# A gated MLP in sums and differences: raw groups and their sums in one tile, signs moved, and some loads placed elsewhere

## The chip, the cores and the metric

The kernel runs on one core of a Trainium2 chip. The time is the device time of one execution in microseconds. A core has five engines that run side by side and wait for each other by semaphores: TensorE (PE, matmuls, with its weight loads PEld), VectorE (DVE), ScalarE (ACT), GpSimd (POOL) and SyncE (SP). SP, ACT and POOL start DMA transfers. Each engine works through its instructions in a fixed order; an instruction that waits holds up all that stand behind it on its engine.

## The reference

```python
x = A_u                                               # 2048 tokens x 576
sa, ca, ga, sb, cb, gb = silu(c) @ w_mod              # six rows of 576
h = layernorm(x) * (1 + ca) + sa
x = x + ga * ssm(h)                                   # long convolution over the tokens
h = layernorm(x) * (1 + cb) + sb
z = gelu(h @ w_in)                                    # 576 -> 4608
z1, z2 = z[:, :2304], layernorm(z[:, 2304:])
g = w_sp @ z2 + b_sp[:, None]                         # 2048 x 2048, over the tokens
x = x + gb * ((z1 * g) @ w_out)                       # 2304 -> 576
```

The convolution and the layer norms stand as in the reference. The change is in the second half, from `z` on.

## The kernel before, in words

**Stages.** The first 440 us compute the convolution; its result is x1, kept in device memory as `x1_d`, 16 blocks of 128 rows. Phase A (`phase_a`, about 440 to 694 us) makes z2 for all 2048 tokens, normalises it and stores it as `z2_d`; it also splits `w_in` into float16 parts (`win_d`) and prepares seven of the eight blocks of `w_sp` for the first quarter. Phase B (`phase_b`, to the end) goes through four quarters q of 512 tokens. A quarter has nine steps f. Each makes z1 for 256 of the 2304 columns (`z1_unit` in quarter 0; `z1_pair` in quarters 1 to 3) and then `g = w_sp @ z2` for the same columns (`g_products`), whose result `g_unit` multiplies by z1. After the ninth step `out_block` multiplies by `w_out` in eight halves (four blocks of rows, two halves of columns), adds x1 and stores the rows.

**Seven products in place of eight.** A matrix product is cut into 2 x 2 parts and done as seven products of sums and differences of the parts. So each operand needs seven pieces: four raw groups or three of them, and sums. Each piece is split into two float16 numbers, a high part and a remainder, and three products of these are added: 21 matmuls for a pair of operand tiles. `z2_build` makes a set of z2 (`zset`), `wsp_build` a block of `w_sp` (`wsp`), `n2_build` the rows of the layer norm (`n2o`), and `wa_unit` a set of `w_in` (`zset` again, quarter 1; quarters 2 and 3 load what quarter 1 stored in `wa_d`). Each of them loads four groups of 256 columns into a tile `raw` (four buffers of 4 KB a partition), makes three or four sums on DVE into a tile `sum` (two buffers), and splits raw groups and sums apart: ACT scales to the high part, DVE subtracts it for the remainder. `w_sums` and `z_sums` are the sums. Sets of z2 that a later quarter needs are stored in `set_d` by ACT and loaded by POOL.

**w_in's last rows.** 512 of the 576 rows go through the seven products; the last 64 take six plain matmuls with a tile `wr`. In quarter 0 `z1_unit` scales them from its tile `wf` (three buffers) into a tile `ot` with an ACT copy (L1468), stores them in `wr_d` by ACT (L1470), and `wa_unit` loads them in the later quarters.

**Order.** In phase B the order of the instructions on PE and SP is that of the program. On DVE and ACT it is chosen when the kernel is built, except in the handover after each quarter's ninth step (`self.nc = self.last`), where the builds for the next quarter (`n2_build`, `wsp_build`, and `g_unit` of step 8) keep program order on DVE and ACT too. `ahead` is called at each new set: it builds two sets further on, with raw loads three ahead, and in quarter 0 loads and splits a piece of `w_out`. A load into a buffer waits on SP until the last user of that buffer is done, and SP's later loads wait behind it. In the handover SP's order is: rows for `n2_build`, blocks of `w_sp` as raw buffers come free, the bias row, the first sets of the next quarter, and last the rows of x1 (L1582 on), which take raw buffers too.

Line 129 is that of a helper which records all instructions that keep program order, so the trace tells these apart by their tiles. A program's tile `z1` is called `z` in the trace, `z2_d` is `z_d`, `x1_d` is `x_d`.

Of the kernel before, what the change touches and what calls it, by code (L numbers as in the profile page):

```python
# [765 lines left out]
class Mlp:  # L766
    def __init__(self, tc, ctx, I, x1_d, dram, mod_d, acc, out):
# [7 lines left out]
        self.wr_d = dram.tile([9, 128, 2, 2, 128], F16, name="wr_d")  # L775
# [67 lines left out]
    def start(self):  # L843
# [9 lines left out]
        self.sc = mc.tile([128, 96], F32, name="sc")  # L853
# [83 lines left out]
    def scales_sp(self, q, ps=None):  # L937
# [5 lines left out]
        V.tensor_scalar(qcol(q, INV_SP), qcol(q, I_S), 1.0 / 256, None, op0=ALU.mult)  # L943

# [66 lines left out]
    def wsp_load(self, q, i, pool):  # L1011

        t = self.wss[i] = self.bp.tile([128, 4, 256], F32, name="raw", bufs=4) if pool is None else self.norm_tile(pool).rearrange("p (k n) -> p k n", k=4)
        self.wsp_read(t, q, i)
# [11 lines left out]
    def w_sums(self, r, z):  # L1026
        V = self.nc.vector
        V.tensor_tensor(z[:, 0], r[:, 0], r[:, 1], op=ALU.subtract)
        V.tensor_tensor(z[:, 2], r[:, 2], r[:, 0], op=ALU.subtract)
        V.tensor_tensor(z[:, 1], r[:, 2], z[:, 0], op=ALU.subtract)  # L1030
        V.tensor_tensor(z[:, 3], r[:, 3], z[:, 1], op=ALU.subtract)

    def z_sums(self, r, z):
        V = self.nc.vector
        V.tensor_tensor(z[:, 1], r[:, 2], r[:, 0], op=ALU.subtract)
        V.tensor_tensor(z[:, 0], r[:, 1], z[:, 1], op=ALU.add)
        V.tensor_tensor(z[:, 2], r[:, 3], z[:, 1], op=ALU.subtract)

    def raw(self, key):
        t = self.wss[key] = self.bp.tile([128, 4, 256], F32, name="raw", bufs=4)  # L1040
        return t

# [9 lines left out]
    def wsp_sums(self, i):  # L1052
        t = self.wss["b", i]
        self.w_sums(t[:, :4], t[:, 4:])

    def wsp_hi(self, q, i):
        self.hi(self.wsp_tile(q, i)[:, :, 0], self.wss["b", i][:, 1:], self.qcol(q, S_S), act=True)

    def wsp_lo(self, q, i):
        o = self.wsp[q, i]  # L1060
        self.lo(o[:, :, 1], self.wss.pop(("b", i))[:, 1:], self.qcol(q, S_S), o[:, :, 0])


    def wsp_build(self, q, i):
        r = self.wss.pop(("b", i))
        o = self.wsp_tile(q, i)
        z = self.bp.tile([128, 4, 256], F32, name="sum", bufs=2)
        self.w_sums(r, z)
        for t, k in ((r[:, 1:], slice(0, 3)), (z, slice(3, 7))):
            self.split(o[:, k, 0], o[:, k, 1], t, self.qcol(q, S_S), act=True)  # L1070

    def z2_load(self, n):
        self.nc.sync.dma_start(self.raw(("a", n)), self.z2_d[n // 4, n % 4].rearrange("p s g c -> p s (g c)"))

    def z2_build(self, n):
# [4 lines left out]
        z = self.bp.tile([128, 4, 256], F32, name="sum", bufs=2)  # L1080
        self.z_sums(r, z)
        for t, k in ((r, slice(0, 4)), (z[:, :3], slice(4, 7))):
            nc.scalar.activation(o[:, k, 0], t, AF.Copy)  # L1083
            nc.vector.tensor_tensor(o[:, k, 1], t, o[:, k, 0], op=ALU.subtract)  # L1084
# [20 lines left out]
    def roots(self, z=None, x=None):  # L1105
# [10 lines left out]
        if z is not None:  # L1116
            r2 = ap.tile([128, 1], F32, name="r2")
            nm = ap.tile([128, 1], F32, name="nm2")
            V.tensor_scalar(r2, r[:, 1:2], 256.0, None, op0=ALU.mult)
# [250 lines left out]
    def n2_load(self, q, j):  # L1370
# [4 lines left out]
        t = self.n2t[j] = self.raw(("n", j)).rearrange("p k n -> p (k n)").bitcast(F16).rearrange("p (t m c) -> p t m c", t=4, m=4)  # L1375
        self.nc.sync.dma_start(t, self.n2_d[q][:, :, j:8:2])

    def n2_build(self, q, j):

        V, t, o = self.nc.vector, self.n2t.pop(j), self.n2o[q][j]  # L1380
        r = self.bp.tile([128, 4, 256], F32, name="sum", bufs=2)
        for h in range(2):
            V.tensor_tensor(r[:, 2 * h:2 * h + 2].rearrange("p k (t c) -> p (k t) c", c=128), t[:, :, h], t[:, :, 2 + h], op=ALU.add)
        z = self.bp.tile([128, 4, 256], F32, name="sum", bufs=2)
        self.w_sums(r, z)
        for u, k in ((r[:, 1:], slice(0, 3)), (z, slice(3, 7))):
            self.split(o[:, k, 0], o[:, k, 1], u, 0.25, act=True)

    def wa_raw(self, f):
        t = self.raw(("w", f)).rearrange("p (s h) (j c) -> p s h j c", h=2, j=2)  # L1390
# [5 lines left out]
    def wa_unit(self, q, f):  # L1396

        nc, V = self.nc, self.nc.vector
        wr = self.wrs[f] = self.fp.tile([128, 2, 2, 128], F16, name="wr", bufs=2)
# [392 lines left out]
```

## Time and profile before

| What | us |
|---|---|
| three runs | 1803.0, 1799.34, 1793.21 |
| their median | 1799.34 |
| the profiled execution | 1795.97 |
| its span, first to last instruction | 1794.2 |

Busy time of the engines in five stretches of the profiled execution, in us:

| Stretch | length | PE | DVE | ACT | granted clock |
|---|---|---|---|---|---|
| convolution, 0 to 440 | 440.0 | 356.6 | 360.4 | 323.5 | 0.94 |
| phase A, to 693.8 | 253.8 | 241.6 | 231.0 | 165.8 | 0.96 |
| quarter 0, to 925.6 | 231.8 | 223.2 | 192.9 | 122.4 | 0.99 |
| its output and the handover, to 987.6 | 62.0 | 55.5 | 51.2 | 22.8 | 0.94 |
| quarters 1 to 3, to the end | 806.6 | 801.9 | 442.2 | 207.8 | 1.00 |

The granted clock is TensorE's, as a share of full speed. A row of the timeline has the start in us, the length, the engine (a `q` behind it: its queue, where it starts a DMA), the line, the operation, the tile written and the tiles read, the shape, and how many equal ones were merged; in brackets how long the engine stood idle before it and what ended that. A row of the groups has the count, the busy time, the mean in ns, and the idle time before.

### The profile page before, as it was taken

To read this page: it belongs to the slowest core of one execution; us is meant where nothing else is said; L and a number is where in the kernel's file an instruction comes from. 1 tells how busy PE (TensorE), PEld (TensorE's weight loads), DVE (VectorE), ACT (ScalarE), POOL (GpSimd) and SP (SyncE) were. 2 spreads that over 40 slices of the span, in tenths; PEclk is the share of its full clock that TensorE was granted. 3 is DMA by queue.
4 is the path that set the end of the run, shared out by engine and by line. 5 is a ranking of instruction groups with operands and counts; after the bars stand their busy time and mean duration, and the time that the engine had idled before them with its cause. 6 is when DMAs were issued, how large, how long until landed. Compare 5 with 4: busy or idle time off the path is not lost.

```text
span 1794.2 us, 35815 instructions
## 1 busy us (share of the span) xinstructions
PE 1678.7 (94%) x14766; PEld 1251.7 (70%) x14766; DVE 1277.5 (71%) x2522; ACT 842.3 (47%) x1130; POOL 237.5 (13%) x376
## 2 busy tenths in 40 slices
PE   2588999998899998999998999999999999999998
PEld 1244555565455544877786888888888888888887
DVE  8876999966999996989798576778344468344432
ACT  2668999954577665555443343334122123111110
POOL 3311222333122211000000000000111100111100
PEclk9789999998999999999999999999999999999999
DMA  9465746679689888877664787874666573556630
GB/s 250 122 215 183 193 120 172 179 206 305 205 263 280 240 233 241 294 270 256 234 196 155 236 279 269 289 258 129 218 229 211 199 247 106 197 194 209 222 104 27
DMA packets 184757, 378.22 MB, mean 211 GB/s; under 512 B 37681, under 2 KB 105265, under 8 KB 183825
## 3 DMA queue, kind: packets, MB, share of 16 engines
q1 hardware_dynamic: 138384, 157.31, 30.3%
q0 software_dynamic: 36128, 171.57, 29.0%
q10 hardware_dynamic: 10080, 47.04, 6.6%
q8 instruction: 116, 1.90, 0.5%
q14 instruction: 49, 0.39, 0.1%
HBM read 263.94 MB, written 102.49 MB: 204 GB/s over the span
## 4 chain that ended last, share of the span: by engine, by line
PE 55%; DVE 14%; DMA 6%; issue 4%; ACT 3%; POOL 0%; SPq 0%; ACTq 0%; DVEq 0%; POOLq 0%
PE ps L129 49%; PE pz L129 2%; DVE zset L1084 2%; DVE bsz L129 1%; DMA wf<-win_d 1%; DVE n L129 1%; DVE wso L129 1%; DVE wsp L129 1%; DVE rq L129 1%; DVE sum L129 1%; ACT zset L1083 1%; PE pk L487 1%; DMA wst<-in_w_in 1%; DMA wsst<-in_w_out 1%; DVE gt L1517 1%
## 5 line engine op out<-in xcount | busy, mean ns | idle before, releaser
L129 PEld LDWEIGHTS <-zset 128*128 128x128 f16 x7182 | 703.3, 98 | 88.5 <-DVE zset L1084 2.4
L129 PE MATMUL ps<-wsp,zset 128*128 128x256 f16 x6048 | 667.8, 273 | 4.0 <-DVE zset L1084 2.1
L129 PE MATMUL pz<-wz,nt 128*128 128x512 f16 (+1 forms) x1120 | 224.6, 361 | 9.3 <-DVE nt L129 5.0
L129 PEld LDWEIGHTS <-nt 128*128 128x128 f16 x1120 | 109.9, 99 | 117.9 <-issue 7.0
L1517 DVE SCALAR_TENSOR_TENSOR gt<-ps,sc,bsp 128x512 f32<-128x512 f32 x32 | 24.0, 749 | 231.1 <-PE ps L129 231.1
L129 PE MATMUL ps<-wout,z 128*128 128x288 f16 x1344 | 172.3, 288 | 6.5 <-ACT ot L1566 5.7
L1479 POOL DMA_DIRECT2D zset<-set_d x96 | 51.1, 532 | 882.1 <-PE ps L129 594.6
L129 PEld LDWEIGHTS <-z 128*128 128x128 f16 x1344 | 132.5, 99 | 41.1 <-issue 7.0
L1444 ACT ACTIVATE z<-ps 128x256 f32<-128x256 f32 x42 | 13.9, 382 | 245.4 <-PE ps L129 245.4
L129 PE MATMUL ps<-n2o,zset 128*128 128x256 f16 x1134 | 128.2, 273 | 0.0
L1517 DVE SCALAR_TENSOR_TENSOR gt<-ps,sc,gt 128x512 f32<-128x512 f32 (+1 forms) x160 | 108.4, 695 | 4.6 <-DVE gt L1517 0.5
L1084 DVE TENSOR_TENSOR zset<-raw,zset 128x1024 f16<-128x1024 f32 x48 | 58.6, 1221 | 40.0 <-ACT zset L1083 40.0
L1441 DVE TENSOR_TENSOR z<-ps,z 128x512 f32<-128x512 f32 (+1 forms) x126 | 71.9, 597 | 12.5 <-PE ps L129 9.9
L1083 ACT ACTIVATE zset<-raw 128x1024 f16<-128x1024 f32 x48 | 50.2, 1049 | 58.5 <-PE ps L129 26.3
L129 PE MATMUL ps<-n2q,wf 128*128 128x512 f16 x252 | 57.1, 386 | 4.7 <-DMA wf<-win_d 4.7
L395 DVE SCALAR_TENSOR_TENSOR ft<-ft,ps 128x1024 f32<-128x1024 f32 x36 | 43.8, 1218 | 20.8 <-ACT ft L394 20.8
L129 ACT ACTIVATE z<-pz,sc 128x512 f32<-128x512 f32 (+1 forms) x96 | 52.1, 583 | 11.6 <-PE pz L129 6.1
L1567 DVE TENSOR_TENSOR ot<-ot,ps 128x288 f32<-128x288 f32 x32 | 14.3, 451 | 55.0 <-ACT ot L1566 55.0
L129 ACT ACTIVATE z<-z,nm,r 128x1152 f32<-128x1152 f32 x24 | 31.5, 1342 | 44.4 <-DVE nm L129 27.9
L129 PE MATMUL ps<-wout,z1b 128*128 128x288 f16 x384 | 52.3, 286 | 0.0
L1566 ACT ACTIVATE ot<-ps 128x288 f32<-128x288 f32 x32 | 12.7, 405 | 84.1 <-PE ps L129 67.9
L445 PEld LDWEIGHTS pk<-small,kab 128*64 128x64 f32 x576 | 32.6, 139 | 26.7 <-issue 16.6
(359 smaller groups left out, 2772.5 us busy)
## 6 DMA issues: line engine op xcount, KB each, us to landing
zset<-set_d POOLq DMA_DIRECT2D x96, 896.0 KB, 5.0
set_d<-zset ACTq DMA_DIRECT2D x36, 896.0 KB, 6.4
raw<-z_d SPq DMA_DIRECT2D x48, 512.0 KB, 4.3
raw<-in_w_spT SPq DMA_DIRECT2D x43, 512.0 KB, 5.3
z_d<-z POOLq DMA_DIRECT2D x32, 576.0 KB, 9.5
zset<-wa_d POOLq DMA_DIRECT2D x18, 896.0 KB, 4.9
u_d<-st1o POOLq DMA_DIRECT2D x16, 576.0 KB, 4.7
u<-u_d SPq DMA_DIRECT2D x36, 256.0 KB, 4.7
```

The source lines that it names most:

```text
L129: return self.tc.keep_in_program_order(f(*a, **k))
L395: V.scalar_tensor_tensor(f, f, MAGIC, pa, op0=ALU.subtract, op1=ALU.subtract)
L445: T.matmul(pm[64 * ri:64 * ri + 64, 128 * i:128 * i + 128], kk[:, i], r1[ri], start=True, stop=True, skip_group_check=True)
L487: T.matmul(pm, fwd, u1, start=True, stop=True)
L1083: nc.scalar.activation(o[:, k, 0], t, AF.Copy)
L1084: nc.vector.tensor_tensor(o[:, k, 1], t, o[:, k, 0], op=ALU.subtract)
L1441: V.tensor_tensor(dst, pm, to, op=ALU.add)
L1444: A.activation(g1[:, k], p17[:, 0], AF.Copy)
L1479: self.nc.gpsimd.dma_start(o, self.set_d[n // 4, n % 4])
L1517: V.scalar_tensor_tensor(dst, pm, inv, to, op0=ALU.mult, op1=ALU.add)
L1566: A.activation(ot, pl, AF.Copy, scale=1.0 / 2048)
L1567: V.tensor_tensor(ot, ot, pa, op=ALU.add)
```

## The change

- `raw` holds seven groups (three buffers of 7 KB); the sums are made in the same tile, behind or among the raw groups, and the tile `sum` is gone. The high part and the remainder of all seven are made by one ACT and one DVE instruction each, not two.
- The sums are cut to two or three instructions, one of them 512 wide. For this some pieces have the opposite sign: the norm of even blocks of z2 multiplies by -256 instead of 256, and `g_unit` uses a negative scale (`NEG_SP`) in two of its additions. The list of products is one for all (`PRODUCTS`), with the same number of matmuls.
- w_in's last rows: `z1_unit` no longer scales and stores them, `wr_d` is gone. `wr_load` reads them from `win_d` one step ahead, and `wr_scale` scales them in place on ACT (two copies a step) in quarters 1 to 3.
- Rows of x1 go into a tile of their own, `xo`, and into the buffer of `gt`, in turn. In quarters 0 to 2 the first three blocks of rows are loaded from the handover on, ahead of the next quarter's first sets on SP; `w_out`'s even pieces go through `xo` as well.
- Order: at the start of phase B the eighth block of `w_sp` is loaded and built first. In the handover the first n2 load and the first block come one set later and only one block, not three, is loaded then; `n2_build` of the second half comes after block 0, not after block 2.

```diff
+    def w_sums(self, r):
         V = self.nc.vector
+        V.tensor_tensor(r[:, 4:6], r[:, 1:3], r[:, 0:1].to_broadcast([128, 2, 256]), op=ALU.subtract)
+        V.tensor_tensor(r[:, 0], r[:, 2], r[:, 4], op=ALU.add)
+        V.tensor_tensor(r[:, 6], r[:, 3], r[:, 0], op=ALU.subtract)
+    def z_sums(self, r):
         V = self.nc.vector
+        V.tensor_tensor(r[:, 4], r[:, 2], r[:, 0], op=ALU.add)
+        V.tensor_tensor(r[:, 5:7], r[:, 1:4:2], r[:, 4:5].to_broadcast([128, 2, 256]), op=ALU.subtract)
     def raw(self, key):
-        t = self.wss[key] = self.bp.tile([128, 4, 256], F32, name="raw", bufs=4)
+        t = self.wss[key] = self.bp.tile([128, 7, 256], F32, name="raw", bufs=3)
         return t
+    def half(self, key, k):
+        b = self.bp
+        t = self.wss[key] = (b.tile([128, 2, 512], F32, name="gt", bufs=1).rearrange("p h n -> p (h n)") if k else b.tile([128, D], F32, name="xo"))[:, :D]
+        return t
...
     def wsp_build(self, q, i):
         r = self.wss.pop(("b", i))
         o = self.wsp_tile(q, i)
-        z = self.bp.tile([128, 4, 256], F32, name="sum", bufs=2)
-        self.w_sums(r, z)
-        for t, k in ((r[:, 1:], slice(0, 3)), (z, slice(3, 7))):
-            self.split(o[:, k, 0], o[:, k, 1], t, self.qcol(q, S_S), act=True)
+        self.w_sums(r)
+        self.split(o[:, :, 0], o[:, :, 1], r, self.qcol(q, S_S), act=True)
...
     def z2_build(self, n):
...
-        z = self.bp.tile([128, 4, 256], F32, name="sum", bufs=2)
-        self.z_sums(r, z)
-        for t, k in ((r, slice(0, 4)), (z[:, :3], slice(4, 7))):
-            nc.scalar.activation(o[:, k, 0], t, AF.Copy)
-            nc.vector.tensor_tensor(o[:, k, 1], t, o[:, k, 0], op=ALU.subtract)
+        self.z_sums(r)
+        nc.scalar.activation(o[:, :, 0], r, AF.Copy)
+        nc.vector.tensor_tensor(o[:, :, 1], r, o[:, :, 0], op=ALU.subtract)
...
     def n2_build(self, q, j):
...
-        r = self.bp.tile([128, 4, 256], F32, name="sum", bufs=2)
+        r = self.raw(("m", j))
...
+    def wr_load(self, f):
+        wr = self.wrs[f] = self.fp.tile([128, 2, 2, 128], F16, name="wr", bufs=2)
+        self.nc.sync.dma_start(wr.rearrange("p h k c -> p h (k c)"), self.win_d[f:f + 10:9, :, 8:10].rearrange("h p k c -> p h (k c)"))
+    def wr_scale(self, f):
+        for h in range(2):
+            w, b = self.wrs[f][:, h], R_C + (f + 9 * h) // 4
+            self.nc.scalar.activation(w, w, AF.Copy, scale=self.col(b))
...
     def z1_unit(self, q, f):
...
-        nc.scalar.activation(self.wr0[:, h], w[:, 8:], AF.Copy, scale=self.sc[:, R_C + b:R_C + b + 1])
-        if h == 1:
-            nc.scalar.dma_start(self.wr_d[f % 9], self.wr0)
...
     def g_unit(self, q, f, pg, parts=1):
...
-        add(g1, both(p17[:, 0]), self.bsp[q])
+        add(g1, both(p17[:, 0]), self.bsp[q], neg)
...
-        add(g2, both(p17[:, 1]), g2)
+        add(g2, both(p17[:, 1]), g2, neg)
...
     def wout_load(self, f):
-        t = self.bp.tile([128, D], F32, name="gbs") if f % 2 else self.raw(("out", f)).rearrange("p k n -> p (k n)")[:, :D]
+        t = self.half(("out", f), 0) if f % 2 == 0 else self.bp.tile([128, D], F32, name="gbs")
...
+    def rows_load(self, q, tt):
+        self.nc.sync.dma_start(self.half(("x", tt), tt % 2), self.x1_d[4 * q + tt])
     def out_block(self, q):
...
             if h == 0:
-                xts[tt] = self.raw(("x", tt)).rearrange("p k n -> p (k n)")[:, :D]
-                S.dma_start(xts[tt], self.x1_d[4 * q + tt])
+                if tt > 2 or q == 3:
+                    self.rows_load(q, tt)
...
-            if f == 8 and q < 3 and i == 0:
-                block(q + 1, 3)
+            if f == 8 and q < 3 and i == 1:
+                self.n2_load(q + 1, 0)
+                block(q + 1, 1)
+                self.rows_load(q, 0)
...
-        more(0, AHEAD)
-        self.wsp_read(self.raw(("b", 7)), 0, 7)
-        ready(0, 1)
+        self.wsp_read(self.raw(("b", 7))[:, :4], 0, 7)
+        more(0, 2)
+        self.wsp_build(0, 7)
         for i in range(3, 6):
             self.z1_load(0, order[i])
         ready(0, 2)
-        self.wsp_build(0, 7)
...
                 pg = self.g_products(q, f)
+                if q and f < 8:
+                    self.wr_scale(f + 1)
...
                 if q < 3:
-                    if i == 3:
+                    if i == 1:
                         self.n2_build(q + 1, 1)
                     self.wsp_build(q + 1, i)
-                    block(q + 1, i + 4)
+                    block(q + 1, i + 3 if i > 1 else i + 2)
+                    if i == 1:
+                        self.rows_load(q, 1)
+                        block(q + 1, 4)
             self.nc = self.most
             if q < 3:
+                self.rows_load(q, 2)
+                self.wr_load(0)
                 self.bias_load(q + 1)
+                self.wr_scale(0)
                 ready(q + 1, 2)
             self.out_block(q)
```

82 lines of the change are left out of this document (35 added, 47 removed).

## The prediction

> **What bounds the kernel now.** I read the page's first part, then the waits of PE from 640 us on, then the busy time by stretches, then the timeline at each wait.
>
> ```profile
> span 1794.2 us, 35815 instructions
> ...
> PE 1678.7 (94%) x14766; PEld 1251.7 (70%) x14766; DVE 1277.5 (71%) x2522; ACT 842.3 (47%) x1130; POOL 237.5 (13%) x376
> ...
> PE ps L129 <- ACT ot L1566: 5.7, 1, 5.7
> PE ps L129 <- DMA wf<-win_d: 4.7, 1, 4.7
> PE ps L129 <- DVE zset L1084: 2.1, 1, 2.1
> PE ps L129 <- DVE gt L1517: 1.9, 1, 1.9
> PE ps L129 <- DVE ot L1567: 0.8, 1, 0.8
> ...
> 718.10:907.20 189.10, 185.11 (x1515) 148.79 (x1514) 164.65 (x253) 103.17 (x132) 0.00 (x0) 0.99 0.74 260
> 985.00:1780.00 795.00, 795.00 (x7079) 692.26 (x7078) 439.42 (x728) 206.99 (x276) 59.48 (x112) 1.00 0.60 205
> ```
>
> PE is busy for all of 985 to 1780 us (795.00 of 795.00): there only fewer matmuls could help, and the change keeps their number. What it can win after 640 us is the five waits, 15.2 us, and what follows them:
>
> ```profile
> 707.68:710.60 2.92, 2.92 (x8) 0.51 0.91 271
> 768.80:771.05 2.25, 0.17 (x3) 1.00 0.57 162
> 771.95:775.30 3.35, 3.35 (x19) 0.50 0.48 138
> 810.57:814.00 3.43, 3.43 (x32) 1.00 0.84 289
> 972.56:976.70 4.14, 4.14 (x19) 0.50 0.67 269
> ```
>
> Columns: stretch, length, PE busy (matmuls), granted clock, DMA. After three of the waits PE runs at half clock: about half of 2.92, 3.35 and 4.14 us is lost, 1.5 + 1.7 + 2.1 = 5.3 us; after the 1.9 us wait nothing is. So the prize is 15.2 + 5.3 = 20.5 us, 1.1% of the span, and nothing of it lies in the stretch from 985 us. Now the three places.
>
> **First place, the first z1 products (about 700 us).**
>
> ```profile
> 693.79 6.42 PE L129 MATMUL ps<-n2q,wf 128*128 128x512 f16 x29
> 701.06 0.49 ACT L1468 ACTIVATE ot<-wf,sc 128x256 f16<-128x256 f16 x1
> 701.58 2.26 SPq L129 DMA_DIRECT2D wf<-win_d  x3
> 707.68 10.63 PE L129 MATMUL ps<-n2q,wf 128*128 128x512 f16 x42 [4.66 <-DMA wf<-win_d]
> 710.93 0.69 ACT L1472 ACTIVATE z<-ps,sc 128x512 f32<-128x512 f32 x1 [7.44 <-DMA z_d<-z]
> ...
> DMA to landing us min/median/max: 3.1/7.1/8.9
> ```
>
> The fourth wf tile waits for the first one's buffer. PE is done with that after 14 matmuls of 0.213 us, at 696.8, but ACT's scaling copy (L1468), queued behind the end of the norm, reads it at 701.06; the load goes out at 701.58 and PE gets it at 707.68. The change takes the copy out of this quarter (wr is scaled in place one quarter later), so the load can go out near 696.8 and, 6.1 us later, arrive at 702.9, when PE asks for it. Loads five and six follow at 699.8 and 702.8; with the median landing of wf (7.1 us, last row) each is about 1 us late. I leave 2 us of waits: of 4.7 + 1.5, **4.2 us won**.
>
> Condition: the next consumer. The ACTIVATE at 710.93 waits, by its row, for the store of z2's last block (z_d), because a z1 tile lies on a released z2 tile; all zset conversions stand behind it on ACT. The new tiles (7 groups x 3 instead of 4 groups x 4 plus sums 4 x 2, in KB: 21 instead of 24) move z1 by 3 KB, which may or may not free it. The profile does not show the layout. I take the tile as free, at 0.6: 3 KB is most of a z1 tile of 4 KB. The other answer is rival B.
>
> **Second place, the sets of quarter 0 (718 to 907 us).**
>
> ```profile
> 764.94 0.78 ACT L796 ACTIVATE wout<-raw,sc 128x576 f16<-128x576 f32 x1 [3.70 <-DMA raw<-in_w_out]
> 806.87 0.78 ACT L796 ACTIVATE wout<-gbs,sc 128x576 f16<-128x576 f32 x1 [4.84 <-DMA gbs<-in_w_out]
> ...
> L1084 DVE TENSOR_TENSOR zset<-raw,zset 128x1024 f16<-128x1024 f32 x48 | 58.6, 1221 | 40.0 <-ACT zset L1083 40.0
> L1084 DVE TENSOR_TENSOR zset<-sum,zset 128x768 f16<-128x768 f32 x48 | 45.7, 951 | 0.0
> L1037 DVE TENSOR_TENSOR sum<-raw,sum 128x256 f32<-128x256 f32 x57 | 23.8, 418 | 0.0
> ...
> L129 DVE TENSOR_TENSOR sum<-raw 128x512 f32<-128x512 f16 x12 | 7.7, 685 | 2.9 <-DMA raw<-n_d 2.9
> ...
> L129 ACT ACTIVATE wsp<-xz,sc x7: 1788/1802/1808, 600.7 to 690.4; 128x1792 f16<-128x1792 f32 x7
> L129 DVE SCALAR_TENSOR_TENSOR wsp<-xz,sc,wsp x7: 2030/2071/2085, 606.4 to 692.2; 128x1792 f16<-128x1792 f32 x7
> ```
>
> Both waits (2.1 and 1.9 us) come after ACT, in order, stood on a w_out load. A set costs DVE 3 x 0.42 + 1.22 + 0.95 = 3.43 us; new: 0.42 + 0.69 + 2.07 (the 1792-wide form, seen in phase A) = 3.18, so 0.25 x 36 = 9 us of DVE, on an engine that has 189.10 - 164.65 = 24.5 us to spare. ACT loses eighteen copies of 0.5 us. The w_out loads get their own tile but are issued at the same steps, so ACT can still stand on them. Bounds: all 5.7 us (2.1 + 1.9 + 1.7 of half clock) to nothing; I take **3.0 us**, half, since the DVE lead grows but the loads that ACT stood on remain.
>
> **Third place, the handover from quarter 0 to 1 (925 to 988 us).**
>
> ```profile
> 916.37 1.28 DVE L129 TENSOR_TENSOR sum<-raw 128x512 f32<-128x512 f16 x2
> 925.97 0.75 DVE L129 SCALAR_TENSOR_TENSOR gt<-ps,sc,bsp 128x512 f32<-128x512 f32 x1
> 933.74 0.76 DVE L129 TENSOR_TENSOR sum<-raw 128x256 f32<-128x256 f32 x2
> 936.37 0.92 ACT L129 ACTIVATE wsp<-raw,sc 128x768 f16<-128x768 f32 x1
> 937.70 0.75 DVE L129 TENSOR_TENSOR sum<-raw 128x256 f32<-128x256 f32 x2
> 941.67 1.29 DVE L129 TENSOR_TENSOR sum<-raw 128x512 f32<-128x512 f16 x2
> ...
> 953.64 2.88 SPq L129 DMA_DIRECT2D raw<-in_w_in  x4
> 958.01 0.43 DVE L1406 TENSOR_TENSOR raw<-raw 128x256 f32<-128x256 f32 x1 [0.42 <-DMA raw<-in_w_in]
> 967.30 13.39 SPq L129 DMA_DIRECT2D raw<-x_d  x4
> 971.21 0.40 PE L129 MATMUL ps<-wout,z 128*128 128x288 f16 x1 [5.74 <-ACT ot L1566]
> 987.61 4.75 PE L129 MATMUL ps<-n2o,zset 128*128 128x256 f16 x42
> ```
>
> Now PE stops because the rows of x1 are loaded only at 967.30: on SP's queue they stand behind w_in's raw tiles, which wait for raw buffers. Their own tiles (xo, gt), loaded ahead of those, remove this: 5.7 + 0.8 + 2.1 = 8.6 us. **What is late next** is the first w set of quarter 1, which PE needs at 987.61 - 8.6 = 979.0.
>
> Its raw buffer comes free later now. In this stretch the operations of the blocks run in program order on DVE and ACT. Today one block takes 941.67 - 937.70 = 3.97 us, because ACT converts the three raw groups (936.37) while DVE still works on the block before. Merged, ACT must wait for all sums and DVE for all of ACT: 2 x 0.42 + 0.69, then 1.80, then 2.07 = 5.40 us (the free output sums, 0.4 us each, fit into the gap); an n2 build, with its two adds (1.29), 6.7. The n2 sums now need a raw buffer too; the last set of quarter 0 frees one at 916.4, when n2's build starts today. On today's clock: n2 916.4 to 923.1, block 0 to 928.5, gate and g_unit (933.74 - 925.97 = 7.8, and 0.6) to 936.9, n2 to 943.6, blocks 1 to 5 to 970.6. With three raw buffers, w's first load takes block 5's: 970.6 instead of 953.64. The first add follows 4.4 us after (958.01 - 953.64), 975.0; four adds, ACT and DVE (1.7 + 1.80 + 2.07 = 5.6) give 980.6 if nothing is in the way, 986.0 with one block (5.4) between. PE waits 1.6 to 7.0 us; I take 4.3 and 1.9 of half clock, 6.2 against 8.6: **2.4 us won**.
>
> By the Trainium skill ("TensorE: Matmul & The Clock Gate", What's actually happening) the clock drops only after an idle window of about 3.4 us; here 2.25 us of idling did it (the rows at 768.80 and 771.95), so the row decides. By that rule a wait under 3.4 us would be free of the 1.9.
>
> **The rest.** 54 scalings of wr (0.5 us each, the copy's row) go to ACT in quarters 1 to 3, which is busy for 206.99 of 795.00 us: hidden; uncovered they would cost at most one 0.5 us each, 27 us. wr's load now reads win_d, one quarter after it was written; it is issued one unit ahead (over 20 us). Sign changes swap a constant for another, at nothing; four tiny NEG_SP operations too. The third and fourth x1 rows must wait for stores of the first two, and on SP wr, bias and w's loads stand behind them; the first is summed and stored after the third of eight output products (6.6 us each, 979.0 - 926 over 8), some 30 us before the last, so I cost this at nothing; if it were 10 us later it would add to the w set's wait. In the handovers to quarters 2 and 3 no w set is built and PE's first need of a block comes later than all eight are done: nothing.
>
> **Sum.** 4.2 + 3.0 + 2.4 = 9.6 us off the profiled execution's 1795.97 (span 1794.2 and 1.8 around it): 1786.4. That execution was 3.4 us under the median of the runs shown, 1799.34; on that median: **1789.7 us**.
>
> **Rivals.**
> - B, the copy goes but ACT still stands on the z_d store: zset's first set is then converted after 711.6, behind block 7, which now comes first: 711.6 + 2 x 1.80 + 2.07 = 717.3 where PE began its products at 718.15. With a half-clock stretch of 1.5 us the first place wins nothing (-0.7); with 1.5 and 2.4 at the others: 3.2 us, 1796. For it: the row at 710.93; against: the moved tiles.
> - C, every wait goes: 20.5 us, 1779. It needs the w set by 979.0, so the chain of blocks must not grow. By the Trainium skill ("VectorE: DVE Perf Modes", Rules for kernel authors: "Minimize op *count*, not sems") it shrinks, as each block has four DVE operations instead of six. From rows: if ACT's 1.80 hid as today, a block would take 3.6 us instead of 3.97 and w's set would come before 971. Against it: no ACT work of the same block is left that could hide.
> - D, slower. Merging makes every set of quarter 0 serial too: sums, ACT 1.80, DVE. Unless DVE fills these gaps with other sets' work it loses up to 36 x 1.80 = 65 us, and it has 24.5 us to spare (plus 9 saved). It decides from about half unfilled: beyond that PE waits. At 85% unfilled, 55 - 33.5 = 21.5 us lost, 6.6 won at the other places: 14.9 slower, 1814. For it: DVE already stood 40.0 us behind ACT's zset halves (first row of the groups); against: these operations have no fixed order, and sums need no zset buffer, so they can be early.
>
> **Chances.** Forecast 0.42 (1785 to 1795), B 0.23, C 0.18, D 0.17. Half a per cent, 9 us, is about what a measurement can tell from no change: 1790.3. Over half of the forecast's cases and C lie below: faster 0.42; the rest of the forecast, B and a mild D: same 0.43; slower 0.15. The range takes in C and leaves most of D out: 1778 to 1804; the likeliest case alone has 1785 to 1795.
>
> **What would show it.** First place: wf loads near 697 us, no PE wait over 2 us before the first set. ACT's gelu that waits for z_d tells B. Handover: x1 rows' loads before w's; one block every 5.4 us, with DVE idle behind ACT; PE's wait on a w zset in place of that on ot. From there to the end PE without a wait; a new wait there, or more than a few us of zset waits in quarter 0, makes the prediction wrong.

## The result, and the profile after

The changed kernel takes 1895.49 us (median of six runs, 1889.84 to 1899.41) against 1797.04 us before (six runs, 1793.21 to 1803.0): ratio 1.0545, 95% interval 1.0517 to 1.0573. It is slower by 98 us; 1789.7 us was forecast and 1804 us was the upper end of the range. The profiled execution took 1892.11 us.

The page of the changed kernel, busy times, four of its groups (count, busy us, mean ns, then the idle time before and what ended it) and one DMA issue (its last number: median us from issue to landing):

```profile
span 1890.2 us, 35620 instructions
...
PE 1702.1 (90%) x14766; PEld 1257.7 (67%) x14766; DVE 1268.3 (67%) x2352; ACT 842.0 (45%) x1078; POOL 236.8 (13%) x376
...
L1091 ACT ACTIVATE zset<-raw 128x1792 f16<-128x1792 f32 x48 | 80.8, 1690 | 83.0 <-DVE zset L1092 40.3
L1092 DVE TENSOR_TENSOR zset<-raw,zset 128x1792 f16<-128x1792 f32 x48 | 96.5, 2019 | 27.1 <-ACT zset L1091 27.1
...
L1036 DVE TENSOR_TENSOR raw<-raw 128x256 f32<-128x256 f32 x48 | 20.3, 423 | 102.4 <-DMA raw<-z_d 87.7
...
L1427 ACT ACTIVATE wr<-wr,sc 128x256 f16<-128x256 f16 x54 | 24.6, 500 | 100.5 <-DMA wr<-win_d 99.0
...
raw<-z_d SPq DMA_DIRECT2D x48, 512.0 KB, 5.3
```

The edit does what it says: DVE has 170 instructions and 9 us of work less, and the long conversions take 1.69 and 2.02 us. But DVE now stands idle 102.4 us before the first sum of a set (L1036), 87.7 of them for the load of its raw tile. In quarter 0 (690 to 960 us) DVE's wait for these loads was 0.8 us before (first row) and is 64.5 us now:

```profile
DVE sum L1035 <- DMA raw<-z_d: 0.8, 1, 0.8
...
DVE raw L1036 <- DMA raw<-z_d: 64.5, 25, 7.4
```

PE's waits from 640 us on, in the changed kernel (us in total, times, longest):

```profile
PE ps L129 <- DVE gt L1525: 43.3, 19, 8.9
PE ps L129 <- DVE zset L1092: 20.2, 10, 5.7
PE ps L129 <- DVE zset L801: 12.0, 5, 7.1
PE ps L129 <- ACT zset L795: 8.1, 1, 8.1
PE ps L129 <- DVE sc L840: 1.9, 1, 1.9
PE ps L129 <- DMA wf<-win_d: 0.8, 1, 0.8
...
```

They sum to 86.3 us, 71 more than the 15.2 us before. The same 14766 matmuls also keep PE busy 23.4 us longer (1702.1 - 1678.7), mostly at the half clock that follows the longer waits (last section). 71 + 23.4 = 94.5 of the 96.1 us between the two profiled executions.

The busy time of two stretches shows where (stretch, length, PE, PEld, DVE, ACT, POOL, granted clock, DMA). Before:

```profile
700.00:960.00 260.00, 251.35 (x2020) 198.33 (x2018) 219.64 (x356) 137.13 (x173) 3.15 (x4) 0.99 0.70 238
960.00:1270.00 310.00, 303.50 (x2666) 261.44 (x2665) 224.85 (x388) 110.86 (x144) 14.34 (x27) 0.99 0.70 236
```

After:

```profile
700.00:960.00 260.00, 221.59 (x1672) 167.92 (x1671) 171.72 (x208) 102.31 (x92) 0.67 (x1) 0.93 0.59 207
960.00:1270.00 310.00, 261.65 (x2184) 217.43 (x2182) 190.96 (x265) 99.44 (x115) 11.70 (x22) 0.92 0.57 194
```

All is lost in quarters 0 and 1, where sets are made, and in the handover between them. PE, DVE, ACT and the DMA engines are all less busy there than before: none of them is held up by its own work; the engines wait for each other in a ring. The timeline of the changed kernel shows one turn of it:

```profile
725.90 2.02 DVE L1092 TENSOR_TENSOR zset<-raw,zset 128x1792 f16<-128x1792 f32 x1
727.94 12.71 SPq L129 DMA_DIRECT2D raw<-z_d  x3
727.95 0.35 ACTq L1504 DMA_DIRECT2D set_d<-zset  x1
728.70 3.28 ACT L1091 ACTIVATE zset<-raw 128x1792 f16<-128x1792 f32 x2 [8.33 <-DVE zset L1092]
735.28 0.43 DVE L1036 TENSOR_TENSOR raw<-raw 128x256 f32<-128x256 f32 x1 [7.37 <-DMA raw<-z_d]
735.74 0.69 DVE L1037 TENSOR_TENSOR raw<-raw 128x512 f32<-128x512 f32 x1
736.35 3.95 DVE L1092 TENSOR_TENSOR zset<-raw,zset 128x1792 f16<-128x1792 f32 x2
738.42 8.78 PE L129 MATMUL ps<-wsp,zset 128*128 128x256 f16 x58 [5.69 <-DVE zset L1092]
```

A remainder ends at 727.92 and frees a tall tile; only then SP can issue the load of the set three further on (727.94). ACT converts two sets until 731.98, so their remainders could run. But DVE's fixed order has the sums of the set that is just being loaded ahead of them: DVE stands 7.37 us, then does those sums, then the two remainders, and PE gets its set 5.69 us late. These remainders free the next tile, and so on. ACT is a link of the ring too: its store of the set (`set_d`, 727.95) waits for the same remainder, and the two conversions at 728.70 stand behind this store. No run moves the store, so its share isn't known.

### The profile page after: what moved, and what is told of

It reads as the page before. It is cut to its first block, busy times and chain, and to the rows that moved or that the text cites. A ratio compares the mean times of both kernels' runs of the same rounds, so it can differ in the third digit from the quotient of the medians.

```text
span 1890.2 us, 35620 instructions
## 1 busy us (share of the span) xinstructions
PE 1702.1 (90%) x14766; PEld 1257.7 (67%) x14766; DVE 1268.3 (67%) x2352; ACT 842.0 (45%) x1078; POOL 236.8 (13%) x376
## 5 line engine op out<-in xcount | busy, mean ns | idle before, releaser
L129 PEld LDWEIGHTS <-zset 128*128 128x128 f16 x7182 | 711.5, 100 | 192.1 <-DVE gt L1525 31.3
L129 PE MATMUL ps<-wsp,zset 128*128 128x256 f16 x6048 | 692.6, 278 | 65.9 <-DVE gt L1525 43.3
L129 PE MATMUL ps<-n2o,zset 128*128 128x256 f16 x1134 | 132.6, 277 | 20.1 <-DVE zset L801 12.0
L1091 ACT ACTIVATE zset<-raw 128x1792 f16<-128x1792 f32 x48 | 80.8, 1690 | 83.0 <-DVE zset L1092 40.3
L1092 DVE TENSOR_TENSOR zset<-raw,zset 128x1792 f16<-128x1792 f32 x48 | 96.5, 2019 | 27.1 <-ACT zset L1091 27.1
L1036 DVE TENSOR_TENSOR raw<-raw 128x256 f32<-128x256 f32 x48 | 20.3, 423 | 102.4 <-DMA raw<-z_d 87.7
L129 ACT ACTIVATE wsp<-raw,sc 128x1792 f16<-128x1792 f32 x24 | 42.9, 1787 | 74.4 <-DVE raw L129 74.4
L129 DVE SCALAR_TENSOR_TENSOR wsp<-raw,sc,wsp 128x1792 f16<-128x1792 f32 x24 | 50.0, 2083 | 29.1 <-ACT wsp L129 28.6
L1427 ACT ACTIVATE wr<-wr,sc 128x256 f16<-128x256 f16 x54 | 24.6, 500 | 100.5 <-DMA wr<-win_d 99.0
L395 DVE SCALAR_TENSOR_TENSOR ft<-ft,ps 128x1024 f32<-128x1024 f32 x36 | 43.8, 1216 | 19.8 <-ACT ft L394 19.8
L1542 ACT ACTIVATE z<-gt 128x1024 f16<-128x1024 f32 x28 | 29.5, 1055 | 60.1 <-DVE gt L1540 60.1
```

What stands on the lines that cost most here:

```text
L129: return self.tc.keep_in_program_order(f(*a, **k))
L395: V.scalar_tensor_tensor(f, f, MAGIC, pa, op0=ALU.subtract, op1=ALU.subtract)
L1036: V.tensor_tensor(r[:, 4], r[:, 2], r[:, 0], op=ALU.add)
L1091: nc.scalar.activation(o[:, :, 0], r, AF.Copy)
L1092: nc.vector.tensor_tensor(o[:, :, 1], r, o[:, :, 0], op=ALU.subtract)
L1427: self.nc.scalar.activation(w, w, AF.Copy, scale=self.col(b))
```

## The experiments

All ratios are against the kernel before, run on the same chip; one hundredth is 18 us. DVE's and ACT's order outside the handovers is chosen anew when a kernel is built, so an edit can move more than itself.

**Tiles of their own.** The changed kernel with four raw tiles of four groups and two tiles of sums again, hence two conversions; all other parts of the change stay:

```diff
-        t = self.wss[key] = self.bp.tile([128, 7, 256], F32, name="raw", bufs=3)
+        t = self.wss[key] = self.bp.tile([128, 4, 256], F32, name="raw", bufs=4)
...
+        return self.bp.tile([128, 3, 256], F32, name="sum", bufs=2)
...
-        nc.scalar.activation(o[:, :, 0], r, AF.Copy)
-        nc.vector.tensor_tensor(o[:, :, 1], r, o[:, :, 0], op=ALU.subtract)
+        for t, k in ((r, slice(0, 4)), (z, slice(4, 7))):
+            nc.scalar.activation(o[:, k, 0], t, AF.Copy)
+            nc.vector.tensor_tensor(o[:, k, 1], t, o[:, k, 0], op=ALU.subtract)
```

> The changed kernel with one part undone: the raw groups have four tiles of 4 KB again and the sums two tiles of 3 KB, so each operand is converted in two parts (groups 0 to 3, then the sums) as before the change. All the rest stays: signs and fewer sums, w_in's last rows scaled later, own room for the rows of x1, the new orders. Theory 1 (buffers: a tall tile is held from its load to the last remainder, and there are three of them): the 90 us of TensorE waits of quarters 0 and 1 go, the gains of the first and third places stay, 1780 to 1792 us. Theory 2 (the merged conversion is serial: ScalarE waits for all sums): the same, this run doesn't tell it from theory 1. Theory 3 (the other parts, above all the loads and scalings of w_in's last rows in quarter 1, cost the time): stays over 1840 us.

Measured: 1790.33 us, ratio 0.9951 (0.9936 to 0.9966), half a per cent faster than the kernel before. PE's waits from 640 us on in this run:

```profile
PE ps L129 <- DVE zset L1099: 3.3, 3, 1.4
PE pz L129 <- DVE nt L129: 3.3, 1, 3.3
PE ps L129 <- DVE gt L1536: 2.7, 3, 2.2
PE ps L129 <- DVE zset L801: 1.9, 2, 1.0
...
```

The whole loss goes when the operand tiles are as before; theory 3 falls. What the other parts add once the tiles are tall comes under "Quarter 1".

**Two parts in the tall tile.** Three tall tiles kept; only the conversion of the sets is cut in two (the same in `wa_unit`); blocks of `w_sp` and the rows of the layer norm are still converted in one piece:

```diff
-        nc.scalar.activation(o[:, :, 0], r, AF.Copy)
-        nc.vector.tensor_tensor(o[:, :, 1], r, o[:, :, 0], op=ALU.subtract)
+        for k in (slice(0, 4), slice(4, 7)):
+            nc.scalar.activation(o[:, k, 0], r[:, k], AF.Copy)
+            nc.vector.tensor_tensor(o[:, k, 1], r[:, k], o[:, k, 0], op=ALU.subtract)
```

> The changed kernel with its three tall tiles, but each set's conversion in two parts again (groups 0 to 3, which wait for the loads and one sum, then groups 4 to 6). Theory 1 (three tiles, held until the last remainder): the tile comes free no earlier, so the loads stay late: 1875 to 1905 us, and VectorE still waits some 60 us for raw tiles between 690 and 960 us. Theory 2 (serial merged conversion): the chain of a set gets shorter by about one ScalarE piece, 0.7 to 1.0 us, and most of the loss goes: 1795 to 1820 us.

Measured: 1876.14 us, 1.0442 (1.0388 to 1.0497). DVE's waits in quarter 0:

```profile
DVE raw L1036 <- DMA raw<-z_d: 61.9, 22, 6.7
```

The wait for raw tiles is about as long as in the changed kernel (64.5 us). One long conversion of a set instead of two costs some 18 us (0.0103) in this state: theory 2 is a small part.

**Sets pinned.** The sets' DVE instructions keep program order (in `z2_build` and in `wa_unit`, where `ahead` calls them):

```diff
...
+        old, self.nc = self.nc, self.pinned if self.inside else self.nc
         nc = self.nc
...
+        self.nc = old
         return o
```

> The changed kernel with one thing different: the VectorE instructions of the sets that are made during the products keep the order of the program (sums of set k, remainder of set k, sums of set k+1), so no sums of a later set that waits for its load stand ahead of the remainder that would free a tile. Theory 1 in its pure form (too few tiles whatever the order): little changes, 1870 to 1900 us. Theory 4 (three tiles would do, but VectorE's queue puts sums that wait for a load ahead of the remainder of a set whose ScalarE part is done, so that one late load holds up the next load as well): the waits for raw tiles fall under 20 us in quarter 0 and the time comes to 1795 to 1840 us.

Measured: 1862.62 us, 1.0365 (1.0335 to 1.0396). DVE's waits in quarter 0:

```profile
DVE zset L129 <- ACT zset L1092: 29.6, 18, 2.7
DVE raw L129 <- DMA raw<-z_d: 19.6, 6, 5.6
```

As theory 4 expected, the wait for the tiles falls under 20 us, so the order has a part in it. But now every remainder stands right behind its own ACT part (29.6 us), and the time lies between the ranges of the two theories.

**Three raw tiles in the kernel before**, nothing else (the same number in `wsp_load`):

```diff
-        t = self.wss[key] = self.bp.tile([128, 4, 256], F32, name="raw", bufs=4)
+        t = self.wss[key] = self.bp.tile([128, 4, 256], F32, name="raw", bufs=3)
```

> The kernel before with three raw tiles of 4 KB where it has four; sums in tiles of their own, conversions in two parts, nothing else changed. Theory 1 (number of tiles): VectorE starts to wait for raw tiles in quarters 0 and 1 as after the change, and at least half of the loss is seen: 1840 us or more. If the tiles matter only because a tall one is held longer (to the remainder of the sums, behind the ScalarE piece of all seven groups), 1797 to 1815 us. Theory 2 (serial conversion): 1797 to 1805 us.

Measured: 1821.36 us, 1.0127 (1.0102 to 1.0153), under what theory 1 asks and over what the others do. PE's waits from 640 us on:

```profile
PE ps L129 <- DMA wf<-win_d: 11.6, 1, 11.6
PE ps L129 <- ACT ot L1566: 6.9, 1, 6.9
PE ps L129 <- DVE gt L1517: 6.1, 6, 1.9
...
```

and DVE's wait in quarter 0:

```profile
DVE sum L1035 <- DMA raw<-z_d: 10.5, 8, 2.3
```

The largest part is lost at the start of phase B (11.6 us against 4.7 before), and DVE's wait for the sets' loads rises from 0.8 to 10.5 us, not to 64.5. So three tiles alone don't make the ring. What else do tall tiles lack? The tile `sum`. It had two buffers, and DVE could not begin the sums of a third set until a remainder gave one back. Theory 5: this kept the sums at two sets ahead, while the loads ran three or four ahead.

**Three and two, three and three.** The kernel with tiles of their own, now with three raw tiles, and then with three tiles of sums as well (each against the run before it):

```diff
-        t = self.wss[key] = self.bp.tile([128, 4, 256], F32, name="raw", bufs=4)
+        t = self.wss[key] = self.bp.tile([128, 4, 256], F32, name="raw", bufs=3)
```

```diff
-        return self.bp.tile([128, 3, 256], F32, name="sum", bufs=2)
+        return self.bp.tile([128, 3, 256], F32, name="sum", bufs=3)
```

> The kernel of the run with tiles of their own (1790.33 us) with three raw tiles of 4 KB instead of four, two tiles of sums kept. Theory 1 (three tiles are too few, since a load takes 5 to 7 us and a tile is held to its remainder): VectorE waits over 40 us for raw tiles in 690 to 960 us as with the three tall tiles, 1860 to 1890 us. Theory 5 (what counts is not the number but how far the sums run ahead of the remainders: two tiles of sums hold the sums at two sets ahead, so that a load that waits for the remainder of set k is needed only one set later; in a tall tile the sums have no tile of their own and can stand right behind the remainder whose tile they need): 1800 to 1825 us, and at most 20 us of such waits.

> The same with three tiles of sums, so 21 KB in all as with three tall tiles, but raw groups and sums in tiles of their own. Theory 5 (sums that can run three ahead, as far as the loads, stand in VectorE's queue right behind the remainder whose tile the load must refill): VectorE's waits for raw tiles come back to 40 us or more in 690 to 960 us and the time goes up to 1840 to 1885 us, although there is one tile more than in the run with three and two. Theory 1 (number of tiles): no slower than with two tiles of sums.

Measured: 1812.26 us, 1.0057 (1.004 to 1.0074), and 1840.46 us, 1.0221 (1.0206 to 1.0236). DVE's waits in quarter 0, with two and with three tiles of sums:

```profile
DVE sum L1036 <- DMA raw<-z_d: 8.9, 5, 3.2
```

```profile
DVE sum L1036 <- DMA raw<-z_d: 33.6, 17, 3.8
```

One tile more, 28 us slower: theory 5, and no number of tiles as such, predicts that. The wait comes back less than expected (33.6 us, where 40 or more were), and the time lies at the lower end of its range. This can be counted in the order of DVE's rows. For each of the 36 sets of quarter 0: how many sets had begun their sums when its own began, itself included, and had not yet run the remainder that frees the raw tile?

| Kernel | at most one | two | three | raw tiles |
|---|---|---|---|---|
| before | 12 | 24 | 0 | 4 |
| tiles of their own | 9 | 27 | 0 | 4 |
| three and two | 11 | 25 | 0 | 3 |
| three and three | 6 | 14 | 16 | 3 |
| two parts, tall | 5 | 17 | 14 | 3 |
| changed | 4 | 17 | 15 | 3 |
| two tokens (below) | 8 | 28 | 0 | 3 |

In the "three" column all tiles are in use: the set's load can start only when the last remainder ahead of its sums ends. A load takes 5.3 us (median, last row of the page above), and DVE stands idle for what the instructions between the two don't fill. In the changed kernel three of the 15 sets have nothing between, and the whole load shows (5.26, 5.62 and 7.37 us). These 15 sets hold 43.5 of the 64.5 us, the 17 of the column "two" 21.0, the four others nothing.

**Late remainder.** Three tall tiles, the order on DVE by hand: sums of set k+1, then the remainder of set k (`later` keeps it until the next set's sums are issued; both are pinned).

```diff
-        nc.vector.tensor_tensor(o[:, :, 1], r, o[:, :, 0], op=ALU.subtract)
+        self.later(lambda: nc.vector.tensor_tensor(o[:, :, 1], r, o[:, :, 0], op=ALU.subtract))
```

> The changed kernel with its three tall tiles and one long conversion per set, but with VectorE's order for the sets written by hand: sums of set k+1, then the remainder of set k, then sums of set k+2, so that neither ScalarE's part nor the load of a tile is waited for right behind what starts it. Theory 5 (order): both waits are mostly gone, 1790 to 1815 us. Theory 1 (three tall tiles are too few in any order): 1850 us or more. Theory 2 (one long conversion is too serial): ScalarE's part of 1.69 us is the next wait, 1820 to 1850 us.

Measured: 1879.03 us, 1.044 (1.0419 to 1.0462): in theory 1's range, not in the others'. But DVE's wait for raw tiles in quarter 0 does fall, from 64.5 to 27.6 us, and PE's longest wait in 690 to 980 us is another:

```profile
PE ps L129 <- DVE zset L129: 31.2, 8, 8.8
```

The held-back remainder is itself late: where `g_unit` comes between, PE waits up to 8.8 us for it. So this order exchanges one wait for another, and the run doesn't tell the theories apart.

**Two tokens.** The constraint itself put back into the changed kernel, for the sets of z2 (`z2_build`; the expectation calls them sets of z1):

```diff
+        k = self.bp.tile([128, 1], F32, name="token", bufs=2)
+        nc.vector.memset(k, 0.0)
...
-        V.tensor_tensor(r[:, 4], r[:, 2], r[:, 0], op=ALU.add)
+        V.scalar_tensor_tensor(r[:, 4], r[:, 2], k, r[:, 0], op0=ALU.add, op1=ALU.add)
...
-        nc.vector.tensor_tensor(o[:, :, 1], r, o[:, :, 0], op=ALU.subtract)
+        nc.vector.scalar_tensor_tensor(o[:, :, 1], r, k, o[:, :, 0], op0=ALU.add, op1=ALU.subtract)
```

> The changed kernel, three tall tiles and one long conversion per set, with one constraint put back that the two tiles of sums used to give: each set of z1 takes one of two one-element tiles (zero) before its sums and gives it up with its remainder, so that in VectorE's queue the sums of set k+2 stand behind the remainder of set k. The cost beside it is one memset of one element per set. Theory 5 (sums that run three ahead expose the load of the tile): VectorE's waits for raw tiles in quarter 0 fall from 64.5 us to under 35 us, and the time to 1830 to 1870 us, most likely 1850 (the run with three and two tiles, 1812.26 us, is out of reach since a tall tile is still held to the end). Theory 1 (the tall tile's hold alone): 1880 us or more.

Measured: 1856.67 us, 1.0303 (1.0275 to 1.0331). DVE's waits in quarter 0:

```profile
DVE raw L1036 <- DMA raw<-z_d: 11.5, 7, 3.1
```

One element per set wins 39 us, although DVE's instructions for a set take 0.18 us longer (0.06 + 0.48 + 0.69 + 2.08): no set is left in the column "three", and what the edit changes beside is the order. The gain lies in quarter 0: from 700 us to the first w set PE's waits fall from 38.4 to 17.3 us. From that set on, where the sets of w_in have no token, they hardly change (48.1 and 43.8 us).

**The other parts.** In the kernel with tiles of their own, the scaling of w_in's last rows at its old place; then the handover, the rows of x1 and w_out's even pieces as before:

```diff
-                    self.wr_scale(f + 1)
...
+        nc.scalar.activation(self.wr0[:, h], w[:, 8:], AF.Copy, scale=self.sc[:, R_C + b:R_C + b + 1])
...
+            nc.scalar.dma_start(self.wr_d[f % 9], self.wr0)
```

```diff
-                    self.rows_load(q, tt)
+                xt = self.raw(("x", tt)).rearrange("p k n -> p (k n)")[:, :D]
...
+                nc.sync.dma_start(xt, self.x1_d[4 * q + tt])
...
-                    block(q + 1, i + 3 if i > 1 else i + 2)
+                    block(q + 1, i + 4)
```

> The kernel with tiles of their own (1790.33 us), with the scaling of w_in's last rows where it was before the change (a copy by ScalarE at each z1 product of quarter 0, stored and loaded again). If the first place of the prediction holds (4.2 us won there, 5.2 by the trace after): 1793 to 1797 us, with TensorE's waits on wf near 700 us back. If that part is worth nothing: 1789 to 1792 us; if the late scalings cost time in quarter 1: under 1788 us.

> The kernel with tiles of their own (1790.33 us), with the handover as before the change: rows of x1 and the even loads of w_out in raw tiles, blocks loaded four ahead, n2 at its old places. If the x1 rows' wait (5.7 us, with its ScalarE part 8.6 us in the prediction) is what the own room wins: 1794 to 1799 us and TensorE's wait of 5 to 7 us at the output of quarter 0 is back. If the scalings alone made the gain: 1789 to 1792 us.

Measured: 1795.88 us, 0.9979 (0.9962 to 0.9996), and 1802.92 us, 1.0012 (0.9997 to 1.0026). PE's waits: with the old scaling,

```profile
PE ps L129 <- DMA wf<-win_d: 6.3, 1, 6.3
```

and with the old handover,

```profile
PE ps L129 <- ACT ot L1585: 10.1, 1, 10.1
```

So the late scaling wins some 5 us (0.0028, and the intervals just touch), as expected; the own room with its handover some 11 us (0.0061), more than expected, with a wait of 10.1 us where 5 to 7 were. Together that is more than the 9 us that this kernel is faster than before; the parts don't simply add, and where the rest goes wasn't looked for.

**Quarter 1.** ACT waits 73.2 us there for the loads of w_in's last rows (below, first row). First the changed kernel with the old scaling (the diff above); then with the load on ACT's own queue instead of SP's; then tokens for the sets of z2 and of w_in (there the token holds the scale), and the old scaling, together:

```diff
-        self.nc.sync.dma_start(wr.rearrange("p h k c -> p h (k c)"), self.win_d[f:f + 10:9, :, 8:10].rearrange("h p k c -> p h (k c)"))
+        self.nc.scalar.dma_start(wr.rearrange("p h k c -> p h (k c)"), self.win_d[f:f + 10:9, :, 8:10].rearrange("h p k c -> p h (k c)"))
```

```diff
...
+        k = self.token()
+        V.memset(k[:, 1:], 0.0)
+        V.tensor_copy(k[:, :1], self.col(S_C))
-        V.tensor_tensor(r[:, 0], r[:, 1], r[:, 0], op=ALU.subtract)
+        V.scalar_tensor_tensor(r[:, 0], r[:, 1], k[:, 1:], r[:, 0], op0=ALU.add, op1=ALU.subtract)
...
-        self.split(o[:, :, 0], o[:, :, 1], r, self.col(S_C), act=True)
+        self.hi(o[:, :, 0], r, self.col(S_C), act=True)
+        self.lo(o[:, :, 1], r, k[:, :1], o[:, :, 0])
```

> The changed kernel with the scaling of w_in's last rows at its old place, all else as changed. In the trace after, ScalarE waits 73.2 us in quarter 1 for the loads of these rows, ahead of the conversions of the sets. Theory 6 (this wait is part of the loss): 1865 to 1885 us, with less TensorE wait in quarter 1. Theory 5 (it is only where ScalarE waits for want of work): the first place's gain of 5 us is lost and nothing is won, 1895 to 1905 us.

> The changed kernel with one word changed: the load of w_in's last rows is issued on ScalarE's queue instead of SP's, where it stood behind loads that wait for a tall tile to come free. Theory 6 (these loads are late because of SP's queue, and ScalarE, waiting for them, holds up the conversions that would free the tiles): ScalarE's wait for them falls under 25 us in quarter 1 and the time to 1870 to 1880 us, the first place's 5 us kept. If the wait is harmless, or the old place won its 17 us by something else: 1890 to 1900 us.

> The changed kernel with three tall tiles and one long conversion, with the two tokens for the sets of z1 and of w_in, and the scaling of w_in's last rows at its old place. The tokens alone won 39 us against the changed kernel (1856.67 us), the old place of the scaling alone 17 us (1878.36 us). If the two are separate causes: 1895 less 56, 1835 to 1845 us. If they are one (the ring of late tiles in quarter 1): 1850 to 1860 us. If the tokens of w_in's sets free quarter 1 as well: 1815 to 1830 us.

Measured: 1878.36 us, 1.0435 (1.0411 to 1.0459); 1888.46 us, 1.0487 (1.0459 to 1.0516); 1833.42 us, 1.0189 (1.0167 to 1.021). The scaling in 980 to 1300 us, in the changed kernel:

```profile
L1427 ACT ACTIVATE wr<-wr,sc 128x256 f16<-128x256 f16 x18 | 8.3, 500 | 73.2 <-DMA wr<-win_d 73.2
```

and with the other queue:

```profile
L1427 ACT ACTIVATE wr<-wr,sc 128x256 f16<-128x256 f16 x18 | 8.1, 496 | 7.6 <-DMA wr<-win_d 7.6
```

Behind loads that wait for tall tiles the small load is late, and ACT, which must convert sets to free these tiles, waits for it. With 66 us of that wait gone the time falls by 7 to 10 us (0.0058), between the two expected ranges: a real part, but most of the 73.2 us was idle time that cost nothing. In the kernel with tiles of their own ACT waits 43.0 us for the same loads in 980 to 1300 us, and PE waits only 4.0 us from the first w set on. The old scaling wins 17 to 20 us; what its other half is stays open. Tokens and old scaling together end at 1833.42 us, between two expected ranges; the two gains added (39 + 17) gave 1839, and by the ratios (0.0242 + 0.0110) 1.0193, where 1.0189 was measured. So they look like separate causes; what the tokens of w_in's sets won of it can't be read from this run.

**The sum of the loss**, step by step in ratios: one raw tile less 0.0106, a third tile of sums (that is, sums that run as far as the loads) 0.0164, the tall tile, which is held until the last remainder, 0.0221, one long conversion 0.0103: 0.0594 from 0.9951 to 1.0545, about 107 us. The third step, the largest, isn't pure: it also merges the conversions of the blocks and gives the rows of the layer norm a raw tile, and with it PE waits 5.24 + 0.88 us for the first w set of quarter 1, where the run with three and three has no such wait. That the hold of the tile is the rest of it is argued, not shown. The sizes hold for this path; along another, with the order restored first, they would be others. Whether long conversions would pay with a fourth tall tile (28 KB, where tiles of their own take 22) wasn't tried.

## Why the prediction was wrong, point by point

**What bounds the kernel, and the prize**: right. With the ring gone the time is 1790.33 us where 1789.7 was forecast, but that is another kernel, and the agreement is partly luck, since its three terms were not of the forecast sizes.

**First place** (4.2 us won): right. The timeline of the changed kernel there:

```profile
695.39 6.36 SPq L129 DMA_DIRECT2D wf<-win_d  x3
...
701.49 0.69 ACT L1482 ACTIVATE z<-ps,sc 128x512 f32<-128x512 f32 x1 [0.98 <-ACT z L1482]
...
708.30 3.19 PE L129 MATMUL ps<-n2q,wf 128*128 128x512 f16 x14 [0.85 <-DMA wf<-win_d]
```

The loads go out from 695.39, PE waits 0.85 us, and ACT doesn't stand on the store of z2 (rival B): z1's first results come by 701.5. Undoing the part costs about 5 us.

**Second place** (3.0 us won): **here the prediction failed.** It priced a set's instructions on DVE (3.18 us forecast; 0.42 + 0.69 + 2.02 = 3.13 measured) and concluded that "the DVE lead grows". It counted what DVE has to do, and not how long a raw tile is held, how many there are, and what DVE's order then puts behind a load. Three tiles were weighed only for the handover. The tile `sum` was seen as room that the change saves; it was also the only thing that kept the sums from running as far ahead as the loads. In its place the runs show DVE standing 64.5 us for raw tiles in quarter 0, against 0.8 before, and 11.5 with the order put back; instead of 3.0 us won, the stretch 700 to 960 us lost 30 us of PE's busy time, and the stretch 960 to 1270 us another 42.

**Third place** (2.4 us won): the mechanism was right, the size wrong. The rows of x1 are early and PE no longer waits for them; a block takes 5.92 us instead of 5.40 (five from 992.97 to 1022.58), and PE waits for the first w set:

```profile
992.97 2.08 DVE L129 SCALAR_TENSOR_TENSOR wsp<-raw,sc,wsp 128x1792 f16<-128x1792 f32 x1 [1.86 <-ACT wsp L129]
...
1018.38 1.91 SPq L129 DMA_DIRECT2D raw<-in_w_in  x4
...
1022.58 2.08 DVE L129 SCALAR_TENSOR_TENSOR wsp<-raw,sc,wsp 128x1792 f16<-128x1792 f32 x1
...
1028.15 0.61 PE L129 MATMUL ps<-n2o,zset 128*128 128x256 f16 x2 [8.07 <-ACT zset L795]
1030.58 5.83 PE L129 MATMUL ps<-n2o,zset 128*128 128x256 f16 x40 [1.82 <-DVE zset L801]
```

8.07 + 1.82 = 9.9 us, against 4.3 taken and 7.0 as the upper end: the place loses instead of winning. The mis-sized term is the time of the set's load: it goes out at 1018.38, 1.7 us before PE, without the wait, would have asked for the set (1028.15 - 8.07), where 8.4 us was forecast (970.6 and 979.0). With tiles of their own the same edit wins about 11 us, since no such wait replaces the old one.

**The rest at nothing**: wrong for quarter 1. "From there to the end PE without a wait" held only from about 1260 us on; before that quarter 1 makes sets of w_in and of z2 in the same ring, and the wr loads, moved behind them on SP, add 7 to 10 us of it.

**Rivals.** C, every wait goes, leaned on the Trainium skill ("VectorE: DVE Perf Modes", Rules for kernel authors), which says to minimise the number of operations. Here the kernel with fewer, longer operations loses to the one with more by 6%, though these two differ in their tiles as well; where the conversion of the sets alone was merged, it cost some 18 us. The runs speak against the rule where the longer operation holds a buffer that a load waits for. The chain of blocks, which C needed no longer than 3.97 us a block, took 5.92. D (0.17) named the right direction and the right engine, but as its mechanism only serial conversions, which the runs price at some 18 us of 107. Its counterargument, that sums "can be early", was the harm itself.

## What to carry to other kernels

A tile's count of buffers does two things: it lets loads run ahead, and it limits how far ahead the compute queue is ordered. When tiles are merged, count for each buffer who frees it last and what stands in the queue between that and the first reader of its next load; if nothing does, the whole load shows. And price a merge by the time it holds the buffer, not only by the instructions it saves.

## What the runs showed of the hardware

The granted clock falls after some of PE's waits and not after others. In the changed kernel 40 matmuls take 4.54 us after a wait of 1.59 us, and 6.53 us after one of 7.15 us:

```profile
1150.02 4.54 PE L129 MATMUL ps<-n2o,zset 128*128 128x256 f16 x40 [1.59 <-DVE zset L801]
...
1216.88 6.53 PE L129 MATMUL ps<-n2o,zset 128*128 128x256 f16 x40 [7.15 <-DVE zset L801]
```

The length of the wait alone doesn't decide. Of two waits of 2.57 and 2.55 us, shortly after each other, only the second is followed by half clock (stretch, length, PE busy, granted clock, DMA):

```profile
856.74 0.83 PE L129 MATMUL ps<-wsp,zset 128*128 128x256 f16 x6 [2.57 <-DVE gt L1525]
860.12 12.09 PE L129 MATMUL ps<-wsp,zset 128*128 128x256 f16 x83 [2.55 <-DVE gt L1525]
...
855.78:859.17 3.39, 0.83 (x6) 1.00 0.98 362
859.19:862.59 3.40, 2.47 (x12) 0.50 0.58 229
```

From 690 us on, the clock in these traces changes only at times that lie whole steps of 3.41 us apart (736.30, 743.13, 780.68, 787.50 us in the changed kernel), and what counts is how long PE stood idle within one step. The first wait lies across two steps, 1.6 us in one and 1.0 in the next; the second step also holds 1.6 us of the second wait, and at its end, 859.18, the clock falls. From 690 to 1290 us, in all the runs, no step with under 1.79 us of idle time lowered a full clock, and none with over 2.03 us left it. (The prediction's 2.25 us is a stretch with 0.17 us of matmuls in it; the idle time was 2.08 us.) The Trainium skill ("TensorE: Matmul & The Clock Gate", What's actually happening) has a free-running window of 3413 ns, and lets the clock fall after an idle window of about 3.4 us. The traces agree with the window; but here some 2 us of idle time within one were enough, so the rows decide. In the changed kernel 24 steps between 690 and 1300 us ran at half clock, in the kernel before 4.
